# The first phase of an attention and MLP kernel in a listed order, with another start and later weights scaled on ScalarE

## The chip, the core and the metric

The kernel runs on one core of one Trainium2 chip. The metric is device time in microseconds (us) of one execution; lower is better. A core has TensorE (PE in the profile) for matmuls, VectorE (DVE), ScalarE (ACT) and GpSimd (POOL) for the work between them, and queues that start DMA transfers, here SyncE's (SP) above all. Each engine works off its own instructions in the order in which they were written; an instruction that waits holds up all that stand behind it on its engine.

## What is computed

```
def phi(x):                      # q and k, scaled by 64 ** -0.25
    proj = x @ omega.T           # 64 -> 128 features, per head
    h = proj - sum(x * x) / 2
    return exp(h - max(h)) / sqrt(m)

kv  = phi(k).T @ v               # per head: 128 x 64
z   = sum(phi(k), over tokens)
x   = (phi(q) @ kv) / (phi(q) @ z + 1e-6)      # 4 x 576 tokens, 8 heads of 64 -> 2304 x 512
xn  = x / rms(x) * rms_g
x   = (silu(xn @ w_gate) * (xn @ w_val)) @ w_out        # d_ff 1536
out = silu(x @ w_in) @ w_out2                            # d_ff 2048
```

Inputs are numbers of 64 bits for the weights (the kernel decodes their two words itself) and of 32 bits for q, k, v and omega.

## The kernel before

Matmuls of the two MLPs run three times for one product: every operand is kept as a rounded high part and a low part, and high x high, high x low and low x high are added (`PASS`). The 2304 tokens are 18 tiles of 128, in four blocks of 512 tokens (one for each batch) and a last one of 256 (the tails of the four batches).

**The first phase** is the attention and, between its steps, the first sweep of the gated MLP (two of the twelve slices of d_ff) for blocks 0 to 2. Everything in it is an `Op`: an engine, a duration, what it depends on, which buffers it claims and frees, and a function that emits the instructions. `run_order` simulates five engines with these durations and emits, at each step, the ready operation that starts first, with ties and near ties broken by a priority (a place in the sequence of units plus `RANK` of the kind). Its result is a fixed order of instructions on every engine. A unit is a piece of q or k of 256 tokens by four heads (or a tail). Its operations are: the load; the squares and two halvings on GpSimd; four transposes on TensorE (L605); a rounded copy on ScalarE (L610) and the low part on VectorE (L614); per half, six projection matmuls with `bd`, which holds omega (L626); the maxima on VectorE (L643); two small steps on VectorE that make the bias (L649, L656); and four exponentials on ScalarE (L668), one group of four per half, 72 groups in all. For k, matmuls with v follow (L694, tile `kv`). For q, the exponentials are flipped by TensorE (L752) and copied (L758), multiplied with `kv` (L777) and divided, and when a tile is complete it is normalised and flipped (L878) into `xs`, the input of the MLP. `part` (L242) is the gate and value product of a block, 12 matmuls in pieces of three; L999 are the output products.

**Weights** are prepared in steps: a load, five decode steps on VectorE (L156 to L167), two additions on GpSimd (L170), for gate and value a third GpSimd operation that multiplies with `rms_g` (L173), the rounded copy on ScalarE (L186) and the low part on VectorE (L189). The six weights of the first sweep and three of the second are prepared in the first phase (`add_weight`), all others by `Prep.tick` in the stream.

**The stream** is all the rest, from 202.7 us on: sweep after sweep over the blocks, with gate product, SiLU on ScalarE (L259), value product, product on VectorE (L265), rounded copy on ScalarE (L235), low part on VectorE (L236). The output products of a block (L296) come after the next block's first gate product; for the block of 256 tokens, a block's outputs come before its second slice. After so many us of TensorE's work (3.2 at first, then 5.5) a `tick` moves each weight in the pipe one step on: low part of the oldest, rounded copy of the next, then decode and GpSimd steps of the newest.

**The start**: omega is loaded (third on SyncE's queue), transposed by TensorE (L1033), scaled by ScalarE into a buffer (L1037), and split into `bd` by two copies on ScalarE (L1042) and two subtractions on VectorE (L1044).

Of the kernel before, what the change touches and what calls it, by code (L numbers as in the profile page):

```python
# [20 lines left out]
def kernel(  # L21
# [20 lines left out]
    P = 128  # L42
# [11 lines left out]


# [118 lines left out]

    def scaled(job):
        return job[2][1] in "gv"
# [17 lines left out]
    class Prep:  # L194
# [36 lines left out]
    W_PRIO, F_PRIO = 500.0, 1000.0  # L231
# [147 lines left out]

    class Op:
        def __init__(self, kind, eng, dur, emit, deps=(), prio=0.0, claim=(), free=(), port=False):
            self.eng, self.dur, self.emit, self.prio = eng, dur, emit, prio + RANK[kind]
# [7 lines left out]
    LAT = {"PE": 0.22, "DVE": 0.15, "ACT": 0.18, "Pool": 0.08, "SP": 2.5}  # L393
    PE_SLOW, TURN = 8.5, 0.12
    SLACK = {"PE": 0, "DVE": 0.05, "ACT": 0.25, "Pool": 0.05, "SP": 0}


    RANK = {
        "pad": -204.1, "ld_vt": -28.8, "ld_om": -36.6, "t_om": 32.4, "s_om": 19.2, "bd_hi": -23.4,
        "bd_lo": 16.7, "ld_g": 223.9, "ld_x.k": -135.3, "ld_x.q": -134.8, "sq.k": 944,  # L400
        "sq.q": 944.8, "half1.k": 49.6, "half1.q": -38.8, "half2.k": 106.6, "half2.q": 107.4,
        "norms.k": 731, "norms.q": 803.6, "ld_v": 128.5, "tr.k": -36.8, "tr.q": -36.1,
        "tr_hi.k": 11.4, "tr_hi.q": -4, "tr_lo.k": 220.2, "tr_lo.q": -42.7, "pj.k": 485.6,
        "pj.q": 485, "mx.k": 550.9, "mx.q": 513.7, "top.k": 32.7, "top.q": -54.9, "nb.k": -151.1,
        "nb.q": -113.6, "ex.k": 357.7, "ex.q": 357.8, "kv": -389.5, "kvs": 74.8, "fl": -18.7,
        "ev": -25.5, "num": -251.5, "den": 269.3, "rec": 818.1, "mu": 56.7, "ss": 1947.1,
        "rstd": 65, "xn": 1166.2, "xf": -108.5, "x_hi": -29.4, "x_lo": 1103.3, "ld_w": 140,
        "w_dec": 735.3, "w_add": 106.4, "w_hi": -110.4, "w_lo": 763.9, "part": -37.5, "tanh": 354.4,
        "silu": 483.8, "glu": 91.3, "h_hi": -18.2, "h_lo": 40.9, "out": 37.6, "ya": -165.7,
    }  # L410
# [11 lines left out]
    def run_order():  # L422
        slots = {r: [(0.0, None, k) for k in range(n)] for r, n in SLOTS.items()}
        clock = dict.fromkeys(SLACK, 0.0)
        port, mode = 0.0, False
        succ, count = {}, {}
        ready = {e: [] for e in SLACK}
        for o in ops:
            count[o] = len(o.deps)
            for d in o.deps:  # L430
                succ.setdefault(d, []).append(o)
            if not o.deps:
                ready[o.eng].append(o)
        left = len(ops)
        while left:
            best = None
            for eng, waiting in ready.items():
                cand = []
                for o in waiting:
                    s = max(clock[eng], port) if o.port else clock[eng]  # L440
                    for d in o.deps:
                        s = max(s, d.end + lat(d.eng, eng))
                    if eng == "PE" and o.mode != mode:
                        s += TURN
                    for r in o.claim:
                        if not slots[r]:
                            break
                        s = max(s, min(t + (lat(e, eng) if e else 0.0) for t, e, _ in slots[r]))
                    else:
                        cand.append((s, o))  # L450
                if cand:
                    first = min(s for s, _ in cand) + SLACK[eng]
                    s, o = min((c for c in cand if c[0] <= first), key=lambda c: (c[1].prio, c[0]))
                    if best is None or s < best[0]:
                        best = s, o
            s, o = best
            for r in o.claim:
                n = min(range(len(slots[r])), key=lambda n: slots[r][n][0])
                o.slot[r] = slots[r].pop(n)[2]
            o.emit(o)  # L460
            o.end = clock[o.eng] = s + o.dur * (2 if o.eng == "PE" and s < PE_SLOW else 1)
            if o.port:
                port = o.end
# [4 lines left out]
            ready[o.eng].remove(o)  # L468
            for n in succ.get(o, []):
                count[n] -= 1  # L470
                if not count[n]:
                    ready[n.eng].append(n)
            left -= 1
# [3 lines left out]

# [6 lines left out]
    def fetch(dst, src, kind, b, hf, g, parts=range(2)):  # L484
# [11 lines left out]
        else:  # L496
            nc.sync.dma_start(
# [5 lines left out]

# [24 lines left out]
    place, at = [], 0  # L528
    for u in units:
        place.append(at)  # L530
        at += 1 if len(u[0]) == 2 else 2
    last_k = max(n for n, u in zip(place, units) if u[0][0] == "k")
# [296 lines left out]
    def add_norm(i, key, r, last):  # L829
# [14 lines left out]
        if r == 0:  # L844
            xs_.sq = []
# [274 lines left out]
```

## Time and profile before

| | us |
|---|---|
| median of 3 runs | 998.92 (998.87 to 999.29) |
| the profiled execution, its own time | 998.12 |
| its span, first to last instruction | 996.0 |
| TensorE busy in the span | 979.2 |
| VectorE, ScalarE, GpSimd busy | 575.9, 381.0, 312.7 |
| first phase, to the stream's first matmul | 202.66 |

The profile is of one execution, and the views that are used are these: the page's busy times and its table of DMA issues; busy time of each engine in stretches of the span; groups of instructions by line in a stretch, with their count, busy time and mean duration; waits, which say whom an engine waited for; the timeline, with start, duration and what ended the idle time before; and the chain that ended last. A duration of one instruction includes the part that overlaps the next one, so a row of several in succession tells better what one costs. All durations come from this one execution; its own time stands 0.8 us below the median.

### The profile page before, as it was taken

The numbers are of one execution on the slowest core, as the hardware profiler recorded it, in microseconds if no ns is written. First come the engines' busy times: TensorE is split into PE (matmuls) and PEld (weight loads), VectorE is DVE, ScalarE is ACT, GpSimd is POOL, SyncE is SP. The second block draws the span as 40 slices with busy tenths as digits, with TensorE's granted clock in tenths as the row PEclk, the third lists the DMA queues.
The fourth block names the chain that finished last, engine by engine and source line by source line (L and its number), as shares of the span: only waits on it lengthen the run. The fifth ranks groups of instructions, "written<-read, shape, count | busy, mean of one in ns | idle before, by whom it ended". The sixth has DMA issues, their size and how long they took to land.

```text
span 996.0 us, 15344 instructions
## 1 busy us (share of the span) xinstructions
PE 979.2 (98%) x5999; PEld 835.1 (84%) x5999; DVE 575.9 (58%) x1167; ACT 381.0 (38%) x855; POOL 312.7 (31%) x325
## 2 busy tenths in 40 slices
PE   7998999999999999999999999999999999999998
PEld 6988998888788888888888888888888888888887
DVE  6999998358843346685234683623644644525633
ACT  5999996543221112212112334442322322222321
POOL 7877764236610025453000332312312312201200
PEclk9999999999999999999999999999999999999999
DMA  7554312003210002222000220110200211100023
GB/s 197 148 128 108 106 45 64 22 23 105 85 43 1 1 22 64 80 80 74 1 1 1 64 64 23 62 43 22 85 22 22 68 39 27 59 1 22 21 85 106
DMA packets 69112, 55.58 MB, mean 56 GB/s; under 512 B 26160, under 2 KB 63280, under 8 KB 69040
## 3 DMA queue, kind: packets, MB, share of 16 engines
q1 hardware_dynamic: 69040, 54.60, 18.4%
q8 instruction: 47, 0.77, 0.3%
q14 instruction: 25, 0.20, 0.1%
HBM read 49.87 MB, written 4.72 MB: 55 GB/s over the span
## 4 chain that ended last, share of the span: by engine, by line
PE 89%; DVE 5%; ACT 3%; issue 1%; DMA 0%; SPq 0%; DVEq 0%; ACTq 0%
PE g L242 44%; PE y L329 20%; PE y L296 12%; PE b L626 4%; PE b L242 3%; PE b L999 2%; ACT e L668 2%; PE kv L694 1%; PE b L752 1%; PE b L777 1%; DVE small L643 1%; PE b L605 1%; DVE w L189 1%; PE b L878 1%; DVE m L156 1%
## 5 line engine op out<-in xcount | busy, mean ns | idle before, releaser
L242 PE MATMUL g<-xs,w 128*128 128x512 f32 (+1 forms) x2256 | 468.0, 366 | 0.0
L242 PEld LDWEIGHTS g<-xs,w 128*128 128x128 f32 x2256 | 391.1, 188 | 70.0
L170 POOL TENSOR_TENSOR m<-m,raw 128x512 int32<-128x512 int32 x136 | 190.5, 1401 | 562.3 <-issue 421.4
L236 DVE TENSOR_TENSOR h<-s,h 128x512 fp32r<-128x512 f32 (+1 forms) x134 | 96.9, 724 | 185.1 <-ACT h L235 185.1
L329 PE MATMUL y<-w,h 128*128 128x512 f32 (+1 forms) x870 | 200.8, 388 | 0.0
L329 PEld LDWEIGHTS y<-w,h 128*128 128x128 f32 x870 | 162.2, 188 | 33.2
L235 ACT ACTIVATE h<-s 128x512 fp32r<-128x512 f32 (+1 forms) x134 | 78.7, 588 | 183.3 <-DVE s L265 161.3
L296 PE MATMUL y<-h,w 128*128 128x512 f32 (+1 forms) x648 | 136.0, 366 | 1.3 <-DVE w L189 1.2
L296 PEld LDWEIGHTS y<-h,w 128*128 128x128 f32 x648 | 112.0, 189 | 22.0 <-DVE w L189 1.8
L276 ACT ACTIVATE s<-g 128x512 f32<-128x512 f32 (+1 forms) x80 | 44.4, 556 | 171.0 <-PE g L242 170.9
L340 DVE TENSOR_TENSOR ya<-y,ya 128x512 f32<-128x512 f32 (+1 forms) x91 | 62.1, 684 | 57.9 <-PE y L329 56.6
L186 ACT ACTIVATE w<-m 128x512 fp32r<-128x512 f32 x68 | 42.9, 631 | 116.4 <-POOL m L170 69.0
L307 DVE TENSOR_TENSOR ya<-y,ya 128x512 f32<-128x512 f32 (+1 forms) x80 | 50.1, 634 | 53.5 <-PE y L296 53.3
L668 ACT ACTIVATE e<-b,nb 128x128 f32<-128x128 f32 x272 | 78.5, 418 | 4.7 <-DVE nb L656 4.0
L265 DVE TENSOR_TENSOR s<-s,g 128x512 f32<-128x512 f32 (+1 forms) x54 | 33.8, 626 | 76.8 <-PE g L242 75.1
L626 PE MATMUL b<-bd,hl 128*128 128x256 f32 x432 | 65.2, 295 | 2.8 <-DVE hl L614 1.8
L626 PEld LDWEIGHTS b<-bd,hl 128*128 128x128 f32 x432 | 56.3, 193 | 5.9 <-DVE hl L614 2.5
L189 DVE TENSOR_TENSOR w<-m,w 128x512 fp32r<-128x512 f32 x68 | 55.6, 817 | 0.2 <-ACT w L186 0.2
L643 DVE TENSOR_REDUCE small<-b 128x4 f32<-128x512 f32 x72 | 50.0, 695 | 5.2 <-PE b L626 2.5
L259 ACT ACTIVATE s<-g 128x512 f32<-128x512 f32 (+1 forms) x54 | 29.5, 547 | 59.2 <-PE g L242 59.1
L558 POOL TENSOR_TENSOR sq<-sq 128x256 f32<-128x256 f32 (+2 forms) x80 | 45.0, 579 | 1.9
L554 POOL TENSOR_TENSOR sq<-x 128x512 f32<-128x512 f32 (+1 forms) x40 | 39.0, 982 | 19.1 <-DVE small L649 9.9
(69 smaller groups left out, 737.8 us busy)
## 6 DMA issues: line engine op xcount, KB each, us to landing
raw<-in_moe_w_out_dram SPq DMA_DIRECT2D x28, 512.0 KB, 3.5
raw<-in_moe_w_in_dram SPq DMA_DIRECT2D x16, 512.0 KB, 3.6
raw<-in_moe_w_gate_dram SPq DMA_DIRECT2D x12, 512.0 KB, 3.6
raw<-in_moe_w_val_dram SPq DMA_DIRECT2D x12, 512.0 KB, 3.5
x<-in_k_dram SPq DMA_DIRECT2D x16, 256.0 KB, 3.2
va<-in_v_dram SPq DMA_DIRECT2D x32, 128.0 KB, 3.2
x<-in_q_dram SPq DMA_DIRECT2D x16, 256.0 KB, 2.9
out_dram<-ya SPq DMA_DIRECT2D x15, 256.0 KB, 2.0
```

Of the source, the lines that this page charges most:

```text
L170: tt(out=mi, in0=mi, in1=(low if step == 5 else high).bitcast(I32), op=ALU.add)
L189: nc.vector.tensor_tensor(out=st.t[:, 1, :], in0=st.m.bitcast(F32), in1=st.t[:, 0, :].bitcast(F32), op=ALU.subtract)
L235: nc.scalar.activation(out=ht[:, 0, :], in_=s, func=AF.Copy)
L236: nc.vector.tensor_tensor(out=ht[:, 1, :], in0=s, in1=ht[:, 0, :].bitcast(F32), op=ALU.subtract)
L242: nc.tensor.matmul(out=ps, lhsT=w[:, a, cc * P:(cc + 1) * P], rhs=xs[j][:, c, cc, :], start=(n == 0), stop=(n == 3 * KC - 1),)
L296: nc.tensor.matmul(out=ps, lhsT=wt[1, "o", f][:, a, d * P:(d + 1) * P], rhs=hs[f][:, c, :], start=(n == 0), stop=(n == nn - 1),)
L307: nc.vector.tensor_tensor(out=y[:, d, :], in0=ps, in1=y[:, d, :], op=ALU.add)
L329: nc.tensor.matmul(out=ps, lhsT=hs[f][:, a, t * P:(t + 1) * P], rhs=wt[2, "p", f][:, c, d0:d1], start=(n == 0), stop=(n == nn - 1),)
L340: nc.vector.tensor_tensor(out=o[:, t, d0:d1], in0=ps, in1=o[:, t, d0:d1], op=ALU.add)
L626: nc.tensor.matmul(out=st.ps[r][:, 2 * j:2 * j + 2, :].rearrange("p h m -> p (h m)"), lhsT=st.hl[:, c, 2 * r + j, :], rhs=bd[:, a, :], sta ...
L643: nc.vector.tensor_reduce(out=st.mx[:, G * r:G * r + G], in_=st.ps[r], axis=AX.X, op=ALU.max)
L668: nc.scalar.activation(out=st.e[r][:, h, :], in_=st.ps[r][:, h, :], func=AF.Exp, bias=st.nb[:, G * r + h:G * r + h + 1],)
```

## The change

The operations of the first phase are emitted in the order of a list, `ORDER`, of all 1221 operations, in place of the order that ready operations and `RANK` gave; `run_order` keeps the clock only to choose buffers. Some dependencies are added that the old order had left to the simulation, and the transposes of the first three units no longer wait for the squares.

At the start omega's load is issued from ScalarE's queue, and so is the second load of k. The scaling copy is gone: ScalarE and VectorE read the transposed omega with the factor. TensorE gets eleven matmuls of a zeroed tile whose results nobody reads, five of them ahead of omega's transpose, the others between its first operations.

In the stream, the third GpSimd step of a gate or value weight becomes four ScalarE instructions, one per 128 columns, in the same step as decode and additions. The weights of the first phase keep the GpSimd step.

```diff
+    def w_scale(st):
+        mf = st.m.bitcast(F32).rearrange("p (c f) -> p c f", c=KC)
+        for c in range(KC):
+            nc.scalar.activation(out=mf[:, c], in_=mf[:, c], func=AF.Copy, scale=g_sb[:, c:c + 1])
...
-                    for s in range(8 if scaled(job) else 7):
+                    for s in range(7):
                         w_decode(job, st, s, n)
+                    if scaled(job):
+                        w_scale(st)
...
+    ORDER = [
+        114, 10, 59, 0, 1, 2, 5, 7, 6, 8, 16, 17, 18, 28, 11, 12, 13, 4, 65, 29, 14, 34, 1009, 60,
...
+        for o in (ops[n] for n in ORDER):
+            s = max(clock[o.eng], port) if o.port else clock[o.eng]
             for d in o.deps:
...
-            fetch(w.x, k if kind[0] == "k" else q, *u)
+            fetch(w.x, k if kind[0] == "k" else q, *u, queue=nc.scalar if second else nc.sync)
...
-        tr = Op("tr." + kind[0], "PE", 0.109 * 2 * R, transposes, [w.op, w.sqop], i - 1, ["b", "hl"], [(w.op, "x")])
+        early = len(tr_ops) < 3
+        tr = Op(
+            "tr." + kind[0], "PE", 0.109 * 2 * R, transposes, [w.op] if early else [w.op, w.sqop],
+            ["b", "hl"], [] if early else [(w.op, "x")],
+        )
...
-                nc.scalar.activation(out=bd[rows, 0, cols], in_=su.om[rows], func=AF.Copy)
+                nc.scalar.activation(out=bd[rows, 0, cols], in_=su.pt[rows], func=AF.Copy, scale=scale)
...
+        def warm(n):
+            def emit(o):
+                pt = buf(ps_a, [P, G * P], "b", o.slot["b"])
+                for _ in range(n):
+                    nc.tensor.matmul(out=pt, lhsT=zero[:, 0:P], rhs=zero, start=True, stop=True)
...
-            lambda o: nc.sync.dma_start(
+            lambda o: nc.scalar.dma_start(
                 out=om, in_=omega.rearrange("m (o d) -> m o d", o=1).to_broadcast([P, 2, D])
             ),
...
+        first = idle(5, [])
+        t_om = Op("t_om", "PE", 0.11, flip_omega, [ld_om, first], ["b"])
+        spare = [idle(1, [t_om]) for _ in range(2)]
```

The first place is ScalarE's queue at the start; `om` is omega, `x` a loaded tile of k, `hl` its split transpose, `e` the exponentials. Before:

```order
L1037 ACT_TABLE_LOAD
L1037 ACTIVATE e_144<-b_136 128x128
L1042 ACTIVATE bd<-e_144 64x128 x2
L610 ACTIVATE hl_139<-b_138 128x512
L610 ACTIVATE hl_153<-b_152 128x512
L610 ACTIVATE hl_199<-b_198 128x256
L610 ACTIVATE hl_227<-b_226 128x512
L668 ACTIVATE e_239<-b_166,nb_192 128x128 x4
```

And now, with TensorE's queue at the same time behind it:

```order
L1102 DMA om<-in_omega_dram 128x2x64
L1080 ACT_TABLE_LOAD
L1080 ACTIVATE bd<-b_127 64x128 x2
L644 ACTIVATE hl_134<-b_133 128x512
L526 DMA x_141<-in_k_dram 128x4x128
L644 ACTIVATE hl_157<-b_156 128x512
L644 ACTIVATE hl_191<-b_190 128x512
L702 ACTIVATE e_205<-b_173,nb_197 128x128 x4
```

```order
L1091 MATMUL b_121<-zero 128x512 x5
L1075 MATMUL b_127<-ident,om 128x128
L631 MATMUL b_133<-ident,x_116 128x128 x4
L1091 MATMUL b_148<-zero 128x512
L631 MATMUL b_156<-ident,x_141 128x128 x4
L1091 MATMUL b_162<-zero 128x512
L1091 MATMUL b_167<-zero 128x512
L1091 MATMUL b_169<-zero 128x512
L1091 MATMUL b_171<-zero 128x512
L660 MATMUL b_173<-bd,hl_134 128x256 x6
```

Two loads have moved into ScalarE's queue, the second of them behind the copy `hl_134`, and the transposes of that load, `x_141`, stand ahead of the first projection on TensorE.

The second place is TensorE's queue ahead of the projection for the 61st group of exponentials (the last row of each piece; `w_1` and `w_3` are value weights, `w_0` a gate weight, `xs_90` and `xs_91` the inputs of blocks 0 and 1). Before:

```order
L242 MATMUL b_2505<-xs_90,w_1_1443 128x512 x3
L626 MATMUL b_2514<-bd,hl_2462 128x256 x6
L752 MATMUL b_2531<-ident,e_2499 128x128 x4
L242 MATMUL b_2505<-xs_90,w_1_1443 128x512 x3
L626 MATMUL b_2549<-bd,hl_2462 128x256 x6
L605 MATMUL b_2559<-ident,x_2196 128x128 x4
L626 MATMUL b_2570<-bd,hl_2494 128x256 x6
```

And now:

```order
L246 MATMUL b_2507<-xs_90,w_3_2386 128x512 x6
L790 MATMUL b_2518<-ident,e_2429 128x128 x4
L660 MATMUL b_2523<-bd,hl_2435 128x256 x6
L660 MATMUL b_2532<-bd,hl_2435 128x256 x6
L631 MATMUL b_2539<-ident,x_2375 128x128 x4
L246 MATMUL b_2507<-xs_90,w_3_2386 128x512 x6
L246 MATMUL b_2586<-xs_91,w_0_880 128x512 x9
L790 MATMUL b_2604<-ident,e_2406 128x128 x4
L631 MATMUL b_2610<-ident,x_2514 128x128 x4
L919 MATMUL b_2618<-ident,xt_2196 128x128 x4
L660 MATMUL b_2628<-bd,hl_2540 128x256 x6
```

Before, block 0 is in its third product there; now it is through its fourth, and block 1 in its first.

The third place is ScalarE's queue in the stream, from the first output copies of block 3 to the rounded copy of the last block's second slice (`ya` output copies, `w` rounded weights, `m` decoded weights, `s` the SiLU, `h` the rounded copy). Before:

```order
L305 ACTIVATE ya_3574<-y 128x512
L186 ACTIVATE w_3_3693<-m_3626 128x512
L305 ACTIVATE ya_3574<-y 128x512 x3
L186 ACTIVATE w_4_3731<-m_3695 128x512
L259 ACTIVATE s<-g 128x256
L235 ACTIVATE h<-s 128x256
```

And now:

```order
L309 ACTIVATE ya_3592<-y 128x512
L189 ACTIVATE w_3_3714<-m_3644 128x512
L176 ACTIVATE m_3716<-m_3716,g_sb 128x128 x4
L309 ACTIVATE ya_3592<-y 128x512 x3
L189 ACTIVATE w_4_3755<-m_3716 128x512
L176 ACTIVATE m_3757<-m_3757,g_sb 128x128 x4
L263 ACTIVATE s<-g 128x256
L239 ACTIVATE h<-s 128x256
```

Four scaling copies of the weight that is being decoded now stand ahead of the SiLU and the rounded copy; before, that weight's first ScalarE instruction came a step later.

## Rows read from the trace of the kernel before

**Rows 1.** The page: engine busy us (share, instructions), and a DMA issue.
```profile
PE 979.2 (98%) x5999; PEld 835.1 (84%) x5999; DVE 575.9 (58%) x1167; ACT 381.0 (38%) x855; POOL 312.7 (31%) x325
...
x<-in_k_dram SPq DMA_DIRECT2D x16, 256.0 KB, 3.2
```
**Rows 2.** Busy us (instructions) of PE, PEld, DVE, ACT, POOL in a stretch.
```profile
14.15:132.80 118.65, 112.72 (x1593) 104.80 (x1592) 109.17 (x298) 113.64 (x353) 91.70 (x134) 1.00 0.48 127
```
**Rows 3.** The chain that ended last: start, us, engine and line.
```profile
96.30 2.14 PE b L626 x18
...
156.77 2.75 PE b L242 x12
...
190.11 5.44 PE b L999 x24
```
**Rows 4.** TensorE's groups, 14.15 to 129.74: busy us, mean ns, idle before.
```profile
L626 PE MATMUL b<-bd,hl 128*128 128x256 f32 x343 | 50.3, 290 | 2.3 <-DVE hl L614 1.3 <-DVE rd L790 0.3 <-ACT e L668 0.3
```
**Rows 5.** TensorE's groups, 129.74 to 202.66.
```profile
L242 PE MATMUL b<-xs,w 128*128 128x512 f32 x111 | 28.0, 398 | 0.0
L999 PE MATMUL b<-h,w 128*128 128x512 f32 x72 | 16.9, 391 | 0.0
```
**Rows 6.** ScalarE's waits, 14.15 to 132.8: us in total, times, longest.
```profile
ACT e L668 <- DVE nb L656: 3.3, 6, 1.0
```
**Rows 7.** Timeline of the start: start, us, what, idle before and its end.
```profile
1.77 0.51 SPq L1051 DMA_DIRECT2D om<-in_omega_dram  x1
...
3.94 2.04 POOL L554 TENSOR_TENSOR sq<-x 128x512 f32<-128x512 f32 x2 [1.58 <-DMA x<-in_k_dram]
...
5.17 0.45 PE L1033 MATMUL b<-ident,om 128*128 128x128 f32 x1 [5.17 <-DMA om<-in_omega_dram]
...
8.32 2.72 PE L626 MATMUL b<-bd,hl 128*128 128x256 f32 x11 [0.46 <-DVE hl L614]
...
14.15 3.21 ACT L668 ACTIVATE e<-b,nb 128x128 f32<-128x128 f32 x12
```
**Rows 8.** Timeline of ScalarE, 127 to 133: the 61st group.
```profile
131.78 1.20 ACT L668 ACTIVATE e<-b,nb 128x128 f32<-128x128 f32 x4
```
**Rows 9.** Timelines of VectorE, GpSimd, ScalarE and TensorE, 200 to 260.
```profile
220.40 1.42 DVE L156 TENSOR_SCALAR m<-raw 128x512 uint32<-128x512 uint32 x1
...
225.25 2.75 POOL L170 TENSOR_TENSOR m<-m,raw 128x512 int32<-128x512 int32 x2 [1.09 <-ACT s L259]
...
246.74 3.00 POOL L170 TENSOR_TENSOR m<-m,raw 128x512 int32<-128x512 int32 x2 [2.48 <-issue]
...
224.74 0.37 ACT L259 ACTIVATE s<-g 128x256 f32<-128x256 f32 x1
...
227.56 3.04 PE L296 MATMUL y<-h,w 128*128 128x256 f32 x24
...
250.35 6.64 PE L296 MATMUL y<-h,w 128*128 128x512 f32 x28 [1.20 <-DVE w L189]
```
**Rows 10.** Timeline of all engines, 402 to 418.
```profile
405.18 2.76 POOL L170 TENSOR_TENSOR m<-m,raw 128x512 int32<-128x512 int32 x2 [5.47 <-issue]
...
408.02 1.04 POOL L173 TENSOR_TENSOR m<-m,g_sb 128x512 f32<-128x512 f32 x1
...
412.70 0.91 DVE L236 TENSOR_TENSOR h<-s,h 128x256 fp32r<-128x256 f32 x1 [0.48 <-ACT h L235]
...
414.18 3.04 PE L296 MATMUL y<-h,w 128*128 128x256 f32 x24
```
**Rows 11.** Timeline of all engines, 429.5 to 437.
```profile
430.48 2.69 POOL L170 TENSOR_TENSOR m<-m,raw 128x512 int32<-128x512 int32 x2 [3.09 <-issue]
...
431.67 0.63 ACT L235 ACTIVATE h<-s 128x512 fp32r<-128x512 f32 x1 [2.33 <-DVE s L265]
...
433.40 3.92 PE L296 MATMUL y<-h,w 128*128 128x512 f32 x16
433.64 1.52 DVE L189 TENSOR_TENSOR w<-m,w 128x512 fp32r<-128x512 f32 x1
```

More of the change, by code (lines that the diff above doesn't have):

```diff
@@ L423, in run_order @@
         slots = {r: [(0.0, None, k) for k in range(n)] for r, n in SLOTS.items()}
[L424 to L429, printed above, removed]
-            for d in o.deps:
[L431 to L456, printed above, removed]
+        clock, port, mode, queue = dict(FIRST), 0.0, False, 0.0
+        assert sorted(ORDER) == list(range(len(ops)))
+        for o in (ops[n] for n in ORDER):
+            s = max(clock[o.eng], port) if o.port else clock[o.eng]
+            for d in o.deps:
+                s = max(s, d.end + lat(d.eng, o.eng))
+            if o.eng == "PE" and o.mode != mode:
+                s += TURN
             for r in o.claim:
                 n = min(range(len(slots[r])), key=lambda n: slots[r][n][0])
-                o.slot[r] = slots[r].pop(n)[2]
+                t, e, o.slot[r] = slots[r].pop(n)
+                s = max(s, t + (lat(e, o.eng) if e else 0.0))
             o.emit(o)
             o.end = clock[o.eng] = s + o.dur * (2 if o.eng == "PE" and s < PE_SLOW else 1)
+            if o.eng == "SP":
+                o.end = queue = max(queue, s + LAND) + o.xfer
             if o.port:
@@ L677, in add_unit, with add_products @@
         if kind[0] == "k":
[L678 removed]
+            add_kv(u, st, exs)
         else:
[L680 removed]
+            evs = [add_flip_e(st, r, exs[r]) for r in range(R)]
             num = None
             for r in range(R):
[L683 to L685 removed]
+                num = add_q(u, st, r, evs, num)
+    def add_products(b, g, jobs, deps, dur, free):
+        first = (b, g) not in kvfirst
         acc = kvfirst.setdefault((b, g), State())
+        acc.n = 1 if first else acc.n + 1
+        end = acc.n == 3
         def accumulate(o):
@@ L701, in accumulate @@
                     )
-            if i == last_k and end:
+            kv_left.pop()
+            if not kv_left:
                 open_early()
-        o = Op("kv", "PE", dur, accumulate, deps + [kvprev.get((b, g))], i - 1, ["kv"] if first else [], free)
+        kv_left.append(1)
+        o = Op("kv", "PE", dur, accumulate, deps + [kvprev.get((b, g))], ["kv"] if first else [], free)
         kvprev[b, g] = o
-        kv_ops.append(o)
         if first:
@@ L1064 @@
-        for n, u in zip(place, units):
-            add_unit(u, n)
+        bd_ops += spare
+        g_op = Op("ld_g", "SP", 0.5, lambda o: nc.sync.dma_start(out=g_sb, in_=rms_g.rearrange("(c p) -> p c", p=P)))
+        for u in units:
+            add_unit(u)
+        for n in range(4):
+            pj_ops[n // 2].deps.append(idle(1, [tr_ops[n // 2]]))
         for n, job in enumerate(prep_list(0)):
-            add_weight(job, n, [pj_ops[GATE + n]])
-        for n, job in enumerate(prep_list(1)[:W_EARLY]):
-            add_weight(job, 50 + n, [kv_ops[-1]])
+            add_weight(job, [pj_ops[GATE + n]])
@@ L1070 @@
+        for job in prep_list(1)[:W_EARLY]:
+            add_weight(job, list(kvprev.values()))
         n = 0
```

210 lines of the change are left out of this document (96 added, 114 removed), and 68 rows, old and new, of the table ORDER.

## The prediction

> **What bounds the kernel now.** I read the page first. It calls TensorE busy 98% of the span [rows 1], so a change that only frees another engine can gain nothing where that is true. Then the stages. After the first phase (from 202.7 us on) the only wait of TensorE that the trace shows before the last outputs is one of 1.20 us at 250.35 [rows 9]. So some 790 us are at their floor, and there the change can only lose. The first phase is another matter. In the 118.65 us from the first exponentials to those of the 61st of its 72 groups of four, ScalarE is busy 113.64, VectorE 109.17 and TensorE 112.72 [rows 2]. TensorE's figure flatters. Six projection matmuls in a row take 0.71 us (18 in 2.14 [rows 3]), 0.119 each, but 343 of them are booked with 50.3 us [rows 4], where 343 x 0.119 is 40.8; so over 9 us of "busy" are matmuls that stand and wait. TensorE has room in this stretch, ScalarE (96%) hardly any. Behind it, from 129.74 to 202.66, TensorE still has 111 of the 144 gate and value matmuls and all 72 output matmuls of the first three blocks [rows 5], and it is the bound. The phase is thus bound by ScalarE and the chain around it first, by TensorE afterwards, and what moves feed-forward matmuls ahead shortens it.
>
> **The start.** Before, omega's load is issued at 1.77 behind two loads of k, and TensorE's first instruction waits for it until 5.17 [rows 7]. After, it is ScalarE's first instruction, at the time of the table load before, some 0.7; with the 3.3 us from 1.77 to its landing it is there by 4.0, when the first k is there too (3.94 [rows 7]), and the copy that only scaled it is gone. That would give 1.2 us. But the second k load now stands on ScalarE's queue behind the first tile's rounding copy, and that can't run before about 5.0 (transposes at 4.1, then some 0.9 as the low rate makes them). With the 3.2 us of such a load [rows 1] k lands at 8.2. In TensorE's queue its transposes and four zero matmuls stand ahead of the first projection. At the high rate: 4 x 0.11 + 4 x 0.23 + two projections of 0.71, then the second maximum 0.70, 0.3 for the two small steps and 0.4 between engines: exponentials at 12.4. At the low rate, at which 11 projection matmuls took 2.72 [rows 7], 0.247 each, all TensorE's terms double: 15.2. Before they begin at 14.15 [rows 7]. The ends are -1.8 and +1.1; I take **-1.0**, nearer the high rate, as the zeros keep TensorE at work from 1.5.
> The rows have 0.247 for a matmul at the start and 0.119 from 13 us on, the two levels of 1.2 and 2.4 GHz, and nothing on how the level falls. The Trainium skill, "TensorE: Matmul & The Clock Gate" (What's actually happening), says that the low level is the default, activity lifts it and idling brings it back. TensorE would idle from 5 to 8 here, the zeros ahead of that would be wasted, and by that rule the term would be +1.1 in place of -1.0. No row of this trace shows such a fall.
>
> **The order of the first phase.** By the order, the projection before the 61st exponentials has the same attention work ahead of it in both kernels, but 114 gate and value matmuls behind it before and 87 after: 27 x 0.227 (12 take 2.75 [rows 3]) = 6.1 us moved ahead. Behind that point TensorE needs some 4% more than its matmuls' sum, so **-6.4** if the stretch ahead takes them without getting longer; its room of 9 us says that it can, narrowly. In that stretch ScalarE is idle 5.0 us, 3.3 of them waiting for the bias that VectorE computes last [rows 6]. The new order puts that step directly behind its maxima in 15 of 40 units (6 before). I take **-3.0** of the 5.0; the ends are -5.0 and, if the extra matmuls get in the way, a loss (rival 2). One more rounding copy stands between the first and the 61st exponentials, with waits **+0.7**. At the phase's end, now, the last tiles of block 3 are flipped right before the stream wants that block: copy 0.6, subtraction 0.7 and their handovers, less the 1.1 of matmuls behind, then a chain of normalising with only some 8 us of TensorE's work beside it: **+1.0** (0 to 2.5). Before, the last tile was of block 4, wanted 11 us later. Sum: 8.7 us earlier.
>
> **ScalarE scales later weights.** 17 gate and value weights lose one GpSimd multiplication (1.04 [rows 10]) and get four ScalarE copies of 128x128. Four exponentials of that size take 1.20 [rows 8], its last part beside the next instruction, so about 1.05. The price is not the copy. It stands in ScalarE's queue in the very step in which VectorE decodes and GpSimd adds, so ScalarE waits for GpSimd's end with the SiLU and the rounding copy of the running block queued behind it, and TensorE reads that block soon after. I went through the 17 places with the times before; 14 have slack. Three do not.
> (a) 224 to 253. The copies for the third weight wait for GpSimd's adds, 225.25 + 2.75 = 228.0 [rows 9], or 1.1 sooner as VectorE is held up less. SiLU (at 224.74 before [rows 9]), product, rounding and low part then end at 229.7 to 230.8; TensorE wants them from 227.9 (output matmuls from 227.56 [rows 9]). That is 1.8 to 2.9 us, and VectorE goes on late. Its chain then meets the scaling of the fourth weight: adds 246.74 + 3.00 [rows 9] = 249.75, copies 250.9, rounding 251.5, low part 252.25, low half of the last output weight 252.95. TensorE, which resumed at 250.35, resumes at 253.05: **+2.7** for the whole stretch.
> (b) 403 to 418. Adds end 405.18 + 2.76 = 407.9 [rows 10], copies 409.2, SiLU 409.6, its product and split 411. VectorE's queue has four evictions, a low half and five decode steps next, 4.9 us, so the next split ends at 417.3 to 417.8, not 413.6 (412.70 + 0.91 [rows 10]); TensorE wants it at 414.65, after the first of the output matmuls of 414.18 [rows 10]. **+2.6** (to 3.1).
> (c) 430 to 436. Adds end 430.48 + 2.69 = 433.2; the rounding copy that ran at 431.67 [rows 11] ends at 434.85, the low part 435.55, the last weight's low half 436.25 instead of 433.64 + 1.52 = 435.2. Outputs began at 433.40 [rows 11]. **+1.1**.
> Sum +6.4; bounds 0 and 9.
>
> **The forecast.** -8.7 + 6.4 = -2.3. The profiled run took 998.12 (span 996.0), the median of three is 998.92; so 995.8 by the profiled run and 996.6 by the median. A measurement of this kernel tells about 0.2%, 2.0 us, from no change.
>
> **Rivals.** (1) The stalls are covered. If the copies find ScalarE free at (a) to (c), or VectorE is early enough, 6.4 goes, and with it the wait of 1.20 at 250.35, whose cause is VectorE's low half: 996.6 - 6.4 - 1.2 = 989.0. For it: VectorE's 0.42 us step takes 1.42 at 220.40 [rows 9] beside GpSimd's adds, so each multiplication that goes gives VectorE about a microsecond. The Trainium skill, "SBUF — State Buffer" (two separate sides), says that GpSimd and VectorE lock one port pair for a whole instruction, while ScalarE has its own; by that rule all 17 moves free VectorE, and nothing speaks of ScalarE's queue. Against it: the order on ScalarE is fixed, and its waits are worked out above. Chance 0.25.
> (2) Slower: the 27 matmuls and the zeros don't find TensorE's gaps. The queue runs in order; where a piece stands ahead of a projection whose input is ready, ScalarE's exponentials wait for it one for one. Then the first stretch gets longer by 27 x 0.227 = 6.1, the 3.0 is not won, and -8.7 becomes +0.4: 998.9 + 0.4 + 6.4 = 1005.7. It decides from the point at which the 61st exponentials, at 131.78 before [rows 8], begin after 133 us. For it: VectorE, too, is busy 92% there [rows 2]. Against: the room of 9 us. Chance 0.22.
> (3) Gain and stalls cancel: the matmuls fit, ScalarE's idle time stays. Then 996.6 + 3.0 = 999.6, give or take 1. Chance 0.25.
> The forecast has 0.28.
>
> **The numbers.** Forecast and its own range, 994.9 to 998.3, lie mostly beyond the 0.2% (below 996.9). Faster: rival 1 and 0.22 of the forecast and 0.02 of rival 3, 0.49. Same (996.9 to 1000.9): 0.06 and 0.19, 0.25. Slower: rival 2 and 0.04 of rival 3, 0.26. The range must leave out no more than a tenth on either side: it reaches down to rival 1 and up into the nearer half of rival 2, where only part of the matmuls are in the way: 988.5 to 1004.
>
> **What would show it.** In the profile after, the first exponentials begin near 13 us and the 61st group near 128 to 130; the stream's first matmul is at 194 instead of 202.66. TensorE's waits then name three places in the stream: output matmuls waiting for the split of a block, with ScalarE's SiLU behind four small copies that wait for GpSimd, some 2 us at the two places of 256 columns. The forecast is wrong if those waits are missing (rival 1), if the 61st exponentials are later than 133 (rival 2), or if the first projections take 0.247 a matmul until beyond 12 us (the start's +1.1).

## The result, and the profile after

The changed kernel takes 1004.81 us (median of 6 runs, 1002.96 to 1006.80), the kernel before 998.82 (998.12 to 999.29): the ratio is 1.0062, with a 95% interval of 1.0049 to 1.0075. It is slower by 6.0 us where 2.3 faster was forecast, and 0.8 us outside the range. The profiled run is the slowest of the six, 1006.80 with a span of 1005.0, so its parts sum to more than the medians say; both are given below.

First the engines of the page of after (busy us, share, instructions), to be laid beside [rows 1]:

```profile
PE 988.1 (98%) x6010; PEld 839.6 (84%) x6010; DVE 557.9 (56%) x1168; ACT 398.8 (40%) x922; POOL 291.8 (29%) x308
```

VectorE lost 18.0 us of busy time and GpSimd 20.9, ScalarE gained 17.8, and TensorE, with practically the same matmuls, is busy 8.9 us longer. The waits of TensorE over the whole span (line, what it waited for: us in total, times, longest) name the places:

```profile
PE y L300 <- ACT h L239: 6.1, 3, 2.2
PE b L631 <- DMA x<-in_k_dram: 3.1, 1, 3.1
...
PE y L300 <- DVE h L240: 1.0, 3, 0.5
...
PE g L246 <- DVE xs L933: 0.3, 1, 0.3
```

Three things are new. Output matmuls of the stream (L300) wait for the split of their block, for the rounding copy of ScalarE (L239) three times and for VectorE's low part (L240) three times, 7.1 us. Before, the stream had the one wait of 1.20 [rows 9]. In the start TensorE waits 3.1 us for a load of k. And the stream's second gate matmul waits 0.3 us for a part of its input (`xs`, L933) that VectorE finishes only then.

**The start.** Timeline of the start of after (start, us, what, idle before and its end); the rows of before are [rows 7]:

```profile
5.18 0.78 PE L1091 MATMUL b<-zero 128*128 128x512 f32 x1
...
5.61 0.37 ACTq L526 DMA_DIRECT2D x<-in_k_dram  x1
...
9.08 1.11 PE L631 MATMUL b<-ident,x 128*128 128x128 f32 x4 [3.12 <-DMA x<-in_k_dram]
...
11.70 2.76 PE L660 MATMUL b<-bd,hl 128*128 128x256 f32 x12
...
15.68 2.17 ACT L702 ACTIVATE e<-b,nb 128x128 f32<-128x128 f32 x8
```

ScalarE issues the second k load at 5.61, it lands at 9.08, and the twelve projections behind it take 2.76 us, 0.230 each, twice the 0.119 of [rows 3]. The first exponentials begin at 15.68, where before had 14.15.

**The rest of the first phase.** Two stretches of after, from the first exponentials to those of the 61st group and from there to the stream (columns as in [rows 2]):

```profile
15.68:134.79 119.11, 118.37 (x1638) 110.10 (x1638) 107.23 (x306) 113.58 (x353) 91.61 (x136) 1.00 0.51 132
134.79:198.47 63.68, 63.37 (x568) 53.93 (x565) 46.00 (x116) 48.02 (x120) 28.43 (x35) 1.00 0.15 45
```

Before, they took 117.63 (14.15 to 131.78) and 70.88 (to 202.66). From the first exponentials to the stream it is 182.79 instead of 188.51. The first stretch got 1.5 us longer. ScalarE is busy 113.58 us in it, 112.62 before; TensorE 118.37, 111.70 before. TensorE's figure still contains matmuls that stand and wait: by the reckoning of the prediction, 358 projections x 0.119 are 42.6 us, and 52.1 are booked, 9.5 too many, as before (50.3 against 40.8). So it does not show that TensorE is the bound there. TensorE's projections and two of ScalarE's waits in that stretch:

```profile
L660 PE MATMUL b<-bd,hl 128*128 128x256 f32 x358 | 52.1, 289 | 0.7 <-ACT e L702 0.5 <-DVE nb L690 0.2
...
ACT qT L796 <- PE b L790: 1.8, 3, 0.7
...
ACT e L702 <- DVE nb L690: 0.8, 2, 0.6
```

ScalarE's waits for the bias fell from 3.3 us [rows 6] to 0.8. Its waits for results of TensorE (the row above and three smaller ones) rose from 0.8 to 3.2.

**The stream.** When TensorE's groups begin, from its timelines; the last column is the kernel of the second experiment, which has only the moved scaling:

| TensorE begins | before | after | scaling alone |
|---|---|---|---|
| the stream's first gate matmul | 202.66 | 198.47 | 202.48 |
| gate matmuls after the first break at (a) | 230.43 | 229.68 | 233.14 |
| gate matmuls after the second break at (a) | 256.83 | 258.85 | 262.26 |
| gate matmuls after (b) | 417.06 | 423.25 | 425.45 |
| gate matmuls after (c) | 441.69 | 449.67 | 451.26 |
| end of the last output matmuls | 992.39 | 1001.65 | 1001.96 |

After is 4.2 us ahead when the stream begins, 2.0 behind after (a), 6.2 after (b), 8.0 after (c). The rows at (a), GpSimd, ScalarE and TensorE of after:

```profile
221.49 2.70 POOL L168 TENSOR_TENSOR m<-m,raw 128x512 int32<-128x512 int32 x2 [1.43 <-ACT m L176]
...
245.23 2.68 POOL L168 TENSOR_TENSOR m<-m,raw 128x512 int32<-128x512 int32 x2 [2.49 <-issue]
...
224.23 1.28 ACT L176 ACTIVATE m<-m,g_sb 128x128 f32<-128x128 f32 x4 [0.88 <-POOL m L168]
225.41 0.36 ACT L263 ACTIVATE s<-g 128x256 f32<-128x256 f32 x1
226.26 0.42 ACT L239 ACTIVATE h<-s 128x256 fp32r<-128x256 f32 x1 [0.49 <-DVE s L269]
...
247.94 1.28 ACT L176 ACTIVATE m<-m,g_sb 128x128 f32<-128x128 f32 x4 [4.53 <-POOL m L168]
249.13 0.61 ACT L239 ACTIVATE h<-s 128x512 fp32r<-128x512 f32 x1
...
226.73 3.11 PE L300 MATMUL y<-h,w 128*128 128x256 f32 x21 [1.98 <-ACT h L239]
...
249.79 0.49 PE L300 MATMUL y<-h,w 128*128 128x512 f32 x1 [2.20 <-ACT h L239]
250.52 8.49 PE L300 MATMUL y<-h,w 128*128 128x512 f32 x29 [0.23 <-DVE h L240]
```

GpSimd's additions end at 224.19, the copies begin at 224.23, the SiLU that stood behind them in the queue at 225.41, the block's rounding copy at 226.26, and TensorE, three matmuls into the block, goes on at 226.73. At 247.91 the same happens once more, here with the rounding copy itself behind the copies. The rows at (b) and (c):

```profile
410.33 1.28 ACT L176 ACTIVATE m<-m,g_sb 128x128 f32<-128x128 f32 x4 [5.46 <-POOL m L168]
...
417.95 0.41 DVE L269 TENSOR_TENSOR s<-s,g 128x256 f32<-128x256 f32 x1
...
418.87 0.38 PE L300 MATMUL y<-h,w 128*128 128x256 f32 x1 [1.90 <-ACT h L239]
...
440.00 1.28 ACT L176 ACTIVATE m<-m,g_sb 128x128 f32<-128x128 f32 x4 [3.83 <-POOL m L168]
441.18 0.62 ACT L239 ACTIVATE h<-s 128x512 fp32r<-128x512 f32 x1
```

At (b) the delay reaches TensorE by way of VectorE: the product of the next slice (417.95) stands in its queue behind evictions, a low half and five decode steps. The copies wait for GpSimd at all 17 weights; TensorE loses by it at these places alone, and 0.3 us in the block before (a).

### The profile page after: what moved, and what is told of

The parts are those of the page before. It is cut to its first block, busy times and chain, and to the rows that moved or that the text cites. A ratio compares the mean times of both kernels' runs of the same rounds, so it can differ in the third digit from the quotient of the medians.

```text
span 1005.0 us, 15404 instructions
## 1 busy us (share of the span) xinstructions
PE 988.1 (98%) x6010; PEld 839.6 (84%) x6010; DVE 557.9 (56%) x1168; ACT 398.8 (40%) x922; POOL 291.8 (29%) x308
## 4 chain that ended last, share of the span: by engine, by line
PE 56%; ACT 0%; DVE 0%; issue 0%
PE g L246 30%; PE y L333 20%; PE y L300 6%; ACT m L176 0%; DVE w L192 0%; ACT h L239 0%; DVE ya L344 0%; DVE h L240 0%
## 5 line engine op out<-in xcount | busy, mean ns | idle before, releaser
L240 DVE TENSOR_TENSOR h<-s,h 128x512 fp32r<-128x512 f32 (+1 forms) x134 | 91.9, 686 | 210.3 <-ACT h L239 210.3
L300 PE MATMUL y<-h,w 128*128 128x512 f32 (+1 forms) x648 | 140.6, 372 | 7.4 <-ACT h L239 6.1
L239 ACT ACTIVATE h<-s 128x512 fp32r<-128x512 f32 (+1 forms) x134 | 78.6, 587 | 155.5 <-DVE s L269 133.5
L300 PEld LDWEIGHTS y<-h,w 128*128 128x128 f32 x648 | 114.1, 192 | 30.6 <-ACT h L239 7.4
L702 ACT ACTIVATE e<-b,nb 128x128 f32<-128x128 f32 x272 | 75.7, 403 | 2.4 <-DVE nb L690 1.0
L176 ACT ACTIVATE m<-m,g_sb 128x128 f32<-128x128 f32 x68 | 21.8, 391 | 74.1 <-POOL m L168 74.1
```

The source lines that it names most:

```text
L239: nc.scalar.activation(out=ht[:, 0, :], in_=s, func=AF.Copy)
L240: nc.vector.tensor_tensor(out=ht[:, 1, :], in0=s, in1=ht[:, 0, :].bitcast(F32), op=ALU.subtract)
L300: nc.tensor.matmul(out=ps, lhsT=wt[1, "o", f][:, a, d * P:(d + 1) * P], rhs=hs[f][:, c, :], start=(n == 0), stop=(n == nn - 1),)
L702: nc.scalar.activation(out=st.e[r][:, h, :], in_=st.ps[r][:, h, :], func=AF.Exp, bias=st.nb[:, G * r + h:G * r + h + 1],)
```

## The experiments

All ratios are against the kernel before, run beside them on the same chip (medians 998.4 to 998.8).

**1. The scaling back on GpSimd**, start and order as changed:

```
-                    for s in range(7):
+                    for s in range(8 if scaled(job) else 7):
                         w_decode(job, st, s, n)
-                    if scaled(job):
-                        w_scale(st)
```

> The changed kernel, with the one multiplication of the later gate and value weights back on GpSimd; the start and the new order of the first phase stay. Theory A (the scaling by ScalarE in the step of GpSimd's additions is what costs the stream 13.4 us, 806.5 against 793.3 from the stream's first matmul to the end; the first phase by itself ends 4.2 us earlier, 198.47 against 202.66): 998.8 - 4.2 = 994.6 (993.5 to 995.6), the stream's first matmul near 198.5, no wait of TensorE above 1.3 us in the stream, granted clock 1.00 throughout. Theory B (the new order hands the stream over in another state, and the stalls come from that): waits of about 2 us remain near 225, 248 and 419 and the time stays at 1001 or above.

995.59 us (994.85 to 996.24; ratio 0.9969, 0.9957 to 0.9981): theory A. The stream's first matmul is at 198.85, the only wait of TensorE in the stream above 0.3 us is the old one (1.19 at 247.12), the granted clock 1.00. Moving the scaling therefore costs 1004.8 - 995.6 = 9.2 us, and start and order bring 3.2.

**2. The scaling alone**, put into the kernel before by the same lines the other way round.

> The kernel before, with only the scaling of the 17 later gate and value weights moved to ScalarE, in the same step as the additions; start and order of the first phase as before. Theory A: the same stalls at the same places as after, 4.2 us later: TensorE waits about 2 us near 229, 252 and 423, with lower granted clock behind some of them, and 998.8 + 11 to 13.5 = 1010 to 1012.5. Theory B: 999 to 1001, since the old order hands over as before. My recorded sum of the three places alone would give 1005.

1007.49 us (1007.27 to 1008.74; ratio 1.0092, 1.0075 to 1.0109). Theory A, 8.7 us slower, though below the 11 to 13.5 expected. That range came from the slowest run of after, and it counted 2.2 us that the new start and order lose in the stream by themselves (below). TensorE's timeline shows the breaks at the same three blocks:

```profile
230.18 3.12 PE L303 MATMUL y<-h,w 128*128 128x256 f32 x21 [1.98 <-ACT h L242]
...
253.21 0.50 PE L303 MATMUL y<-h,w 128*128 128x512 f32 x1 [2.20 <-ACT h L242]
...
422.03 0.38 PE L303 MATMUL y<-h,w 128*128 128x256 f32 x1 [1.90 <-ACT h L242]
```

The waits are those of after to 0.01 us, so they don't hang on how the first phase hands over.

**3. The four copies one step later**, right ahead of the rounding copy of the same weight:

```
                     for s in range(7):
                         w_decode(job, st, s, n)
-                    if scaled(job):
-                        w_scale(st)
                 else:
+                    if step == 1 and scaled(job):
+                        w_scale(st)
                     (w_high if step == 1 else w_low)(job, st)
```

> The changed kernel, with the four scaling copies issued one step later, right ahead of the rounding copy of the same weight, so that GpSimd's additions ended about one step before them. Theory A (it is the place in ScalarE's queue, waiting for GpSimd, that costs, not the copies): no wait of TensorE of 2 us in the stream, granted clock 1.00, 993.0 to 994.8, that is e1 or up to 1.2 us better, since the wait on a low half at 250.35 [1.20] may go with GpSimd's multiplications. Theory C (the copies' own 17 x 1.28 = 21.8 us on ScalarE make the product chain late): some waits remain and the time stays at 998 or above.

993.74 us (993.39 to 994.07; ratio 0.995, 0.9936 to 0.9965): theory A, 11.1 below the changed kernel with the same number of copies. ScalarE and TensorE at (a):

```profile
220.80 0.37 ACT L263 ACTIVATE s<-g 128x256 f32<-128x256 f32 x1
221.65 0.42 ACT L239 ACTIVATE h<-s 128x256 fp32r<-128x256 f32 x1 [0.49 <-DVE s L269]
223.41 1.28 ACT L176 ACTIVATE m<-m,g_sb 128x128 f32<-128x128 f32 x4 [1.34 <-POOL m L168]
...
223.60 3.03 PE L300 MATMUL y<-h,w 128*128 128x256 f32 x24
...
245.36 6.65 PE L300 MATMUL y<-h,w 128*128 128x512 f32 x28 [0.52 <-DVE w L192]
```

The copies still wait for GpSimd, but SiLU and rounding copy are through before them, and TensorE reads the block without a break. So the place costs, not the copies. Against experiment 1 this is 1.85 us faster by medians. In the profiles the stream is 1.2 us shorter, 1.0 of it at 245, where the wait of [rows 9] shrinks to 0.52; the other 0.7 is a stream that begins earlier (198.18 against 198.85), and that need not come from the scaling: the start is the same in both, and TensorE's wait for the k load there was 3.7 us in the one profiled run and 2.8 in the other.

**4. The second k load early**, on the kernel of experiment 1:

```
-        114, 10, 59, 0, 1, 2, 5, 7, 6, 8, 16, 17, 18, 28, 11, 12, 13, 4, 65, 29, 14, 34, 1009, 60,
+        114, 10, 28, 59, 0, 1, 2, 5, 7, 6, 8, 16, 17, 18, 11, 12, 13, 4, 65, 29, 14, 34, 1009, 60,
...
-            fetch(w.x, k if kind[0] == "k" else q, *u, queue=nc.scalar if second else nc.sync)
+            fetch(w.x, k if kind[0] == "k" else q, *u, queue=nc.sync)
```

> The kernel of e1_scale_gpsimd with the second k load issued by SyncE right behind the first, instead of by ScalarE behind its first rounding copy. Theory D (that place is what makes the start late: TensorE's wait of 3.1 us for this load at 9.08, after which the matmuls run at the low rate again): the wait goes, the first exponentials begin at 12.4 to 13.2 instead of 15.68, the stream's first matmul 2 to 3 us earlier than in e1, total 991.6 to 992.8. Theory E (later waits of ScalarE and VectorE take the start's loss up again): the stream starts within 1 us of e1, total 993.6 to 994.8.

990.65 us (990.37 to 991.18; ratio 0.992, 0.9905 to 0.9935): theory D, and more than it said. The start of this kernel:

```profile
7.61 1.58 PE L658 MATMUL b<-bd,hl 128*128 128x256 f32 x12
...
10.46 2.18 ACT L700 ACTIVATE e<-b,nb 128x128 f32<-128x128 f32 x8 [0.20 <-DVE nb L688]
```

The exponentials begin 5.64 us earlier than in experiment 1 (16.10), the stream 5.65 earlier (193.20): the gain of the start is passed on whole. By medians it is 4.94 (995.59 to 990.65); the profiled run of experiment 1 is the slowest of its six.

**5. Both together.**

> e4_k2_early and e3_scale_late together: scaling by ScalarE one step later, second k load by SyncE behind the first. If the two gains are of separate stages (start and stream), they add: 990.65 - (995.59 - 993.74) = 988.8 (988.3 to 989.3), the only wait of TensorE in the stream about 0.5 us. If they are not separate: 990 or above.

988.99 us (988.83 to 989.37; ratio 0.9904, 0.9887 to 0.992): the gains add. This version beats both kernels, by 9.6 and 15.8 us.

**6. Without the zero matmuls**, on 5:

```
-                for _ in range(n):
+                for _ in range(0):
```

> e5_late_k2 without the ten zero matmuls; nothing that the reference needs is left out. Theory H (the zeros keep TensorE at work through the start, and that keeps its first transposes and projections at the high rate: 12 projections took 1.58 us in e4_k2_early against 2.76 in the changed kernel): without them the 12 take 2.7 or more, the first exponentials come 1 to 2 us later than in e5, total +1 to +2, 989.8 to 990.8. Theory I (the zeros are only in the way, or idle time hides them): within 0.4 us of e5.

989.55 us (989.36 to 989.80), 0.56 above 5: between the theories. The projections do run at the low level, as H says (3.29 us, with some 0.4 of waiting for the low part among them):

```profile
6.23 3.29 PE L660 MATMUL b<-bd,hl 128*128 128x256 f32 x12
...
10.69 2.18 ACT L702 ACTIVATE e<-b,nb 128x128 f32<-128x128 f32 x8
```

But the projections begin 0.95 us earlier (at 7.18 in 5), as no zeros stand ahead of them, and that pays back more than half of it: the first exponentials come 0.67 later than in 5 (10.02). The eleven zero matmuls are worth half a microsecond where the load is early.

**7. Zeros in the gap**, on the kernel of experiment 1:

```
-        def idle(n, deps):
-            o = Op("warm", "PE", 0.21 * n, warm(n), deps, ["b"])
+        def idle(n, deps, more=0):
+            o = Op("warm", "PE", 0.21 * n, warm(n + more), deps, ["b"])
...
-        spare = [idle(1, [t_om]) for _ in range(2)]
+        spare = [idle(1, [t_om], 12 * n) for n in range(2)]
```

> e1_scale_gpsimd (second k load late, as in the changed kernel) with 12 more zero matmuls in TensorE's queue ahead of the second tile's transposes, where TensorE stands idle from 6.0 to 9.1 us; it tells the late load apart from the low rate behind the gap. Theory J (of the 5.65 us that e4 won over e1 some 3.1 are the load itself and the rest the low rate behind the idle time): the 4 transposes, 4 zeros and 12 projections behind the load, 5.9 us of TensorE in the changed kernel, take 3.2, the first exponentials begin 2 to 2.8 us earlier than in e1 (16.10), the total is 995.6 - 2.4 = 993.2 (992.8 to 993.8). Theory K (the rate there does not hang on the gap): first exponentials and total as e1, 995.2 to 996.0, or later by what the zeros take.

993.36 us (993.25 to 993.51; ratio 0.9947, 0.9932 to 0.9962): theory J. TensorE of this kernel:

```profile
5.13 4.26 PE L1089 MATMUL b<-zero 128*128 128x512 f32 x13
9.22 0.60 PE L629 MATMUL b<-ident,x 128*128 128x128 f32 x4
9.58 1.17 PE L1089 MATMUL b<-zero 128*128 128x512 f32 x4
10.59 1.58 PE L658 MATMUL b<-bd,hl 128*128 128x256 f32 x12
```

The load is as late as in experiment 1, but the four transposes take 0.60 instead of 1.11 and the twelve projections 1.58 instead of 2.76; the first exponentials begin at 13.44. Of the 5.64 us between experiments 1 and 4, 2.7 are the low rate behind the idle time and 3.0 the load; by medians 2.2 and 2.7 of 4.9.

**8. The feed-forward pieces nine behind, to the end of the phase**, on 5. A piece of three gate or value matmuls, with what follows it, goes to the place of the ninth piece after it (the two lines that set the place):

```
+            p = max(parts - 1, 0) + k
+            here = at[p] if p < len(at) else len(ORDER)
```

> e5_late_k2 with the feed-forward pieces of the first phase set back by nine pieces of three matmuls each, so that 30 gate and value matmuls stand ahead of the projection of the 61st group of exponentials, as in the kernel before, in place of 57; the attention work keeps its order. It prices the 27 matmuls that the change moves ahead. In the changed kernel the stretch from the first to the 61st exponentials took 119.1 us against 117.6 before, the rest of the phase 63.7 against 70.9. Theory F (TensorE had room: 4.6 of the 6.1 us were free): here the stretch gets 1.5 shorter and the rest 6 to 7 longer, total 4.6 to 5.5 above e5, 993.4 to 994.3. Theory G (TensorE, 118.4 busy of 119.1, is the bound there, so each matmul costs its time wherever it stands): the stretch gets 6 shorter, total within 1 of e5.

1008.88 us (1007.23 to 1010.02; ratio 1.0101, 1.0086 to 1.0116). Neither theory has the total; the stretch up to the 61st exponentials is as F says, 117.41 against 119.41 in 5, so the 27 matmuls, with what follows them, cost it 2.0 where their own time is 6.1. The stretch in 5 and here (columns as in [rows 2]):

```profile
10.02:129.43 119.41, 118.36 (x1634) 109.86 (x1634) 107.45 (x306) 113.76 (x351) 92.31 (x138) 1.00 0.51 131
...
10.34:127.75 117.41, 114.36 (x1607) 105.41 (x1608) 105.60 (x303) 111.73 (x348) 91.55 (x136) 1.00 0.51 134
```

TensorE's busy time falls by 4.0, ScalarE's by 2.0, and ScalarE's idle time stays at 5.7. The three ScalarE instructions that are missing here are the activation of a gate product and two rounding copies, which follow the matmuls that were set back. So the 2.0 are as much as ScalarE's share of what was moved. That is a reading of the busy times; no run moves the matmuls without the ScalarE work behind them.

The rest took 84.24 against 63.69. There the pieces were still behind when the attention work ended, and nothing covered their chains; the largest new wait of TensorE is

```profile
PE b L944 <- ACT xt L935: 3.6, 2, 2.7
```

That part prices the lag at the end, not the 27 matmuls, so experiment 9 lets the pieces catch up.

**9. The 27 matmuls right behind**, all in its old place by the 66th exponentials:

```
+        pj = [i for i, n in enumerate(ORDER) if ops[n].kind[:2] == "pj"]
+        stop = pj[60]
...
-            key.append((max(here, i), 1, i, n))
+            key.append((max(min(here, stop), i), 1, i, n))
```

> e5_late_k2 with the nine pieces of three matmuls (and the small operations that follow them) moved from ahead of the projection of the 61st exponentials to right behind it, and everything in its old place again by the 66th; unlike e8_ff_behind, where the pieces stayed nine behind to the end of the phase. Theory F (of the 27 matmuls' 6.1 us some 4 were free in the stretch, as e8's stretch of 117.4 against 119.4 says): the stretch from the first to the 61st exponentials is 2 shorter, the rest of the phase 6 longer, total 992.5 to 993.5. Theory G (they cost their time wherever they stand): total within 1 us of e5. Theory N (behind it the exponentials wait for them, and the chain to the last tiles gets longer by more than their time): 994 or above.

992.78 us (992.60 to 993.25), 3.8 above 5: theory F by its total. Its split is different. The 59th exponentials begin 109.6 us after the first, 2.3 sooner than in 5; then the 27 matmuls stand in one piece between two projections of one tile, and the 61st exponentials wait for them:

```profile
123.64 0.95 PE L687 MATMUL b<-bd,hl 128*128 128x256 f32 x6
124.43 6.28 PE L246 MATMUL b<-xs,w 128*128 128x512 f32 x27
130.55 0.87 PE L687 MATMUL b<-bd,hl 128*128 128x256 f32 x6
...
133.78 1.15 ACT L729 ACTIVATE e<-b,nb 128x128 f32<-128x128 f32 x4 [3.54 <-DVE rd L859]
```

Ahead, they and what follows them cost 2.3 us, in one piece here 6.1: moving them ahead gains 3.8.

**10. Omega's load on SyncE**, first there, on 5 (`nc.scalar.dma_start` becomes `nc.sync.dma_start`).

> e5_late_k2 with omega's load as SyncE's first instruction, ahead of the loads of k, instead of ScalarE's first: it prices omega's place, and it takes ScalarE's queue of transfers out altogether. Theory L (the place is worth the issue time that omega takes ahead of k on SyncE, 0.5 us): first exponentials 0.4 to 0.6 later than 10.02, total 989.3 to 989.7. Theory M (the stream's small steps of 0.17 us, 1.5 to 2.2 us in all, that all kernels with the new start show against the kernel before, hang on transfers issued by ScalarE): the stream gets 1.5 to 2.2 shorter and the total falls to 987 to 988.

989.03 us (988.68 to 989.32): as 5, so both theories miss. The first exponentials are 0.27 later and the stream begins at the same time. Which engine's queue issues omega's load first makes no difference; what its place ahead of k is worth was not tested.

## Why the prediction was wrong

By medians the two halves were forecast as -8.7 and +6.4, and measured as -3.2 (experiment 1) and +9.2 (the rest). Both were wrong to the same side, by 5.5 and 2.8. In the profiles the first half is +1.95 at the start, -5.8 from there to the stream and +2.2 in the stream, -1.6 in all; most of the rest up to -3.2 lies in the profiled runs, of which that of experiment 1 is 0.65 above its median and that of before 0.7 below.

**The start, -1.0: wrong in sign.** The prediction saw the load behind ScalarE's rounding copy and had both ends, -1.8 and +1.1, and took the one near the high rate, "as the zeros keep TensorE at work from 1.5". They keep it at work only until 5.96; then it idles 3.1 us, the load landing 0.9 later than worked out, and what follows runs at half the rate. Measured: +1.5 in after, +1.95 in experiment 1. The step that failed is that choice: it asked what ran at 1.5 us, not what ran just ahead of the projections, though it had itself worked out that TensorE would idle from 5 to 8. The rule cited there from the Trainium skill, "TensorE: Matmul & The Clock Gate" (What's actually happening), that idling brings the low level back, gave +1.1. The matmuls of the trace agree, though its granted clock does not show the fall (last section), and experiment 7 shows by itself that the rate hangs on the idle time (0.230 to 0.132 a projection).

**The order, -6.4 - 3.0 + 0.7 + 1.0 = -7.7: the direction right, the size -5.7.** From the first exponentials to the stream it is 182.8 us in after, in experiment 4 and in 7, 188.5 before. The 27 matmuls were moved and gained 3.8 (experiment 9). The step that failed is that the prediction moved matmuls alone. The pieces take their activations and rounding copies along, and these went into the stretch that the prediction itself had called bound by ScalarE; they stand in its sum at nothing. Moving the pieces ahead cost 2.0 to 2.3 us there (experiments 8 and 9), about as much as ScalarE's part of them; that it is this part, and not the matmuls, was argued and not tested. The -3.0 for ScalarE's idle time did not come either. The waits for the bias did fall, by 2.5, as the order meant them to; but waits for TensorE's results took their place (0.8 to 3.2), and ScalarE is idle 5.5 of 119.1 us in after, 5.0 before. So the stretch went from 117.6 to 119.1 where 115.3 was forecast. The rest fell by 7.2 where 5.4 was forecast: the +1.0 of draining is not seen there, and some 0.8 more has no name. Half of that +1.0 comes just behind: the stream's first gate product loses 0.5 us, as its second matmul waits for the last tile of its input (199.21 instead of 198.70).

**Something small that the prediction has not.** All kernels with the new start and order lose another 1.6 us in the stream, in steps of 0.07 to 0.09 at some twenty groups of gate matmuls, without a wait; before and experiment 2 don't. With the 0.5 of the first gate product (which experiment 8 does not lose) these are the 2.2 us. Neither the zeros (experiment 6) nor ScalarE's loads (10) cause the steps. Their cause stays open.

**The scaling, +2.7 + 2.6 + 1.1: right in the places, too small at (a).** All three places stall, by the row that was named: copies waiting for GpSimd's additions, SiLU or rounding copy behind them, at (b) with VectorE's queue between. At (b) the low part was said to end at 417.3 to 417.8 and TensorE to lose 2.6 to 3.1; with the scaling alone it lost 2.96. At (c) 1.1 was forecast and 1.18 measured. At (a) it is 5.6 in both kernels: 0.3 in the block before, 2.6 at the first break, 2.7 at the second. The prediction followed the first break from its own times and then took the second one from the times of before, 253.05 against 250.35, as if GpSimd and VectorE had stood still at their hours while TensorE was late. The decoding is issued between TensorE's products, so everything behind the first break moves with it: with the scaling alone, GpSimd's additions for the fourth weight begin at 248.65, before at 246.74. The second break comes on top, 2.6 and 2.7, not 2.7 together. That is nearly the whole miss of this half. That the second break has the size of the forecast is luck: of its 2.7 us only 1.2 are more waiting (2.20 + 0.23 against 1.20), and some 1.6 are the lower granted clock behind it (0.59 and 0.55, last section), which the prediction put at nothing: 29 output matmuls take 8.49 us there, 28 took 6.64 before [rows 9]. In the profiled run of after the clock costs another 1.5 behind (b), 1.0 in the rest of the block (3.9 against 2.96, with the same waits) and 0.6 in the gate matmuls that follow. Two of after's six runs had a granted clock of 1.000 over the whole span and took 1004.41 and 1004.08, so most of the loss does not need it.

**The rivals.** Rival 2 named 1005.7 and its sign that the 61st exponentials begin after 133 us (134.79), and the time is within 1 us of it. But it comes about otherwise: 1.5 of those 3.0 us are the start's, the matmuls did gain 3.8, and against its +0.4 and +6.4 stand -3.2 and +9.2. Rival 1's reason holds in part. By the Trainium skill, "SBUF — State Buffer" (two separate sides), GpSimd and some of VectorE's instructions take one shared port pair for a whole instruction. Experiment 3 agrees with that: VectorE is busy 562.8 us instead of the 572.6 of experiment 1, and the stream is 1.2 us shorter, once ScalarE's queue is out of the way.

## What to carry over

An instruction that waits for another engine belongs into an in-order queue behind all that the bound engine wants next: one step later, the same four copies turned 9.2 us of loss into 1.85 of gain (1.66 between experiments 4 and 5). When a break is priced, everything that is issued by the bound engine's progress has to be moved with it, so two breaks in a row add up. When matmuls are moved, the work of other engines that follows them moves along and has to be priced in the stretch where it lands. And a transfer issued by a computing engine starts when that engine's queue reaches it; here this cost 2.7 us by medians and the low matmul rate behind it another 2.2 (3.0 and 2.7 in the profiles).

## What the hardware showed beside that

Behind a wait of about 2 us in the middle of dense work the low level of 1.2 GHz (a granted clock of 0.50) came back for a few microseconds, but not each time. TensorE's busy time and granted clock (third column from the right) in after behind the second break at (a) and behind (b):

```profile
250.00:252.00 2.00, 1.77 (x4) 0.59 0.43 149
252.00:254.00 2.00, 2.00 (x6) 0.55 0.04 8
254.00:256.00 2.00, 2.00 (x10) 1.00 0.00 0
420.00:422.00 2.00, 2.00 (x15) 0.76 0.25 16
422.00:424.00 2.00, 2.00 (x9) 0.50 0.61 246
```

Behind the first break at (a), 1.98 us, it stayed at 1.00, and with the scaling alone it fell behind the second (0.50 from 254 to 256) and not behind (b), whose waits were the same. It may be part of the spread of after's runs, whose granted clock over the span was 0.994 to 1.000; the times do not follow it strictly (1002.96 at 0.998, 1004.41 at 1.000), and only one run left a trace. And in the start the granted clock reads 1.00 while the projections run at half rate: from 11 to 13 us of after, where one takes 0.230,

```profile
11.00:13.00 2.00, 2.00 (x10) 1.00 0.00 0
```

so there the rate has to be read from the matmuls themselves.
